# Sliding-window attention and a spectral mix on one core: q and k with nine buffers each, their loads two slots further up in the DMA order

## The chip, the core and the metric

The kernel runs on one core of one Trainium2 chip. The time is device microseconds (us) of one launch, from the first to the last instruction and what lies around them. Several runs are summed up by their median. One execution was taken by the hardware profiler; its engines are named PE (matmuls; PEld is its weight load), DVE, ACT, POOL, and SP, which here only issues DMAs.

## What is computed

q, k and v have the shape (8 batches, 8 heads, 576 positions, 64), in float32. The reference, cut to what matters:

```python
scores = scale * np.matmul(q, k.transpose(0, 1, 3, 2))
mask = (rel >= 0) & (rel < 128)                     # rel = query position - key position
scores = np.where(mask, scores + bias[None], -1e9)  # bias = -slope[head] * |rel|
attn = softmax(scores)
x = np.matmul(attn, v)                              # then heads side by side: (8, 576, 512)
X = np.fft.rfft(x, axis=1)                          # the lowest 64 modes are kept
Yr[m] = Xr[m] @ w_r[m] - Xi[m] @ w_i[m]             # one 512 x 512 pair of weights per mode
Yi[m] = Xr[m] @ w_i[m] + Xi[m] @ w_r[m]
u = x + np.fft.irfft(Y, n=576, axis=1)
out = u + np.maximum(u @ w_ch, 0.0)
```

w_r and w_i have 64 x 512 x 512 float32 values each, 67.1 MB apiece: they are most of what is read from memory.

## The kernel before, in words

**The units.** Two heads fill 128 channels, which the code calls group s (0 to 3). One unit is a group of one batch; there are 32 units, and they are worked in 16 pairs. Pair d holds units 2d and 2d+1. Of each unit q, k and v are loaded by one DMA each (288 KB), so a pair has six loads, called q0, q1, k0, k1, v0, v1 for pair 0 and so on up to q30, q31, k30, k31, v30, v31 for pair 15.

**The slots.** The attention runs in slots n = 0, 1, 2, ...; slots 2d and 2d+1 are those of pair d (`_slot`). A slot makes scores (line 427), exponentials (433) and the mask product (441) of its pair, transposes parts of the pair after it (377, copied out at 387), has POOL cast raw loads of the pair two further on to bf16 (`_cast`, line 367: q in the even slot, k and v in the odd one), and finishes the product with v of the pair before (458, normalised at 476). A cast is the last reader of a raw load; when it is done the load's buffer is free.

**The weights.** After slot 10 the spectrum of group 0 is known, and the products of group 0 with the weights are put between the slots (`_modes`, line 663): 22 tiles of three modes (one has one mode), in order 0 to 21. Each tile has two DMAs (w_r and w_i, 768 KB each, line 611). Tile 0 has a place of its own ("spare"); the others use a ring of three places (`RING`, "wring"). The DMA of tile i has to wait until PE has finished tile i-3. From tile 22 on the weights are those of groups 1 to 3 (line 620, one DMA of 1.5 MB each; products at line 694), in the same ring, until the last stretch of the kernel, which computes the output (lines 728 to 870).

**The order of the DMAs.** All 249 DMAs are issued by SP, one after the other, in the order in which the code calls them: `_load(g, d)` for q, k and v, `_send(g)` for weights. An instruction on SP that waits holds back everything behind it. SP waits for three things: for a free buffer (a POOL cast for q, k and v; PE for weights), and, in every DMA from the ninth on, for the DMA eight places earlier to have landed, since there are eight completion semaphores in turn. So at most eight DMAs are under way.

`_load(g, d)` issues q and k of pair d and v of pair d-1. Before the slots, q and k are called up to pair 7 and v up to pair 6. From slot 8 on, each even slot n calls one more: slot 8 calls q and k of pair 8 with v of pair 7, slot 10 those of pair 9 with v of pair 8, slot 12 those of pair 10 with v of pair 9, and so on. `_send` is called at the end of each slot. From slot 10 on this gives the SP order below (the first weights are of tile 4, which wait for PE to finish tile 1 at the end of slot 10):

```
q18 q19 k18 k19 v16 v17 | tile 4: w_r w_i | q20 q21 k20 k21 v18 v19 | tile 5: w_r w_i | q22 q23 ...
```

q and k have seven buffers each (`QK`, line 24), v has five (`VB`). Load q(i) takes the buffer of q(i-7), load v(i) that of v(i-5).

Of the kernel before, what the change touches and what calls it, by code (L numbers as in the profile page):

```python
# [19 lines left out]
LA = 8  # L20
RING = 3
ROWS = 3
VB = 5
QK = 7
BUSY = 12
TAIL = 2

# [6 lines left out]
def kernel(  # L34
# [16 lines left out]
    g = Ctx()  # L51
# [8 lines left out]
    N = len(units)  # L60
    g.first = [units.index((j, grp[0], 0)) for j, grp in enumerate(GROUPS)] + [N]
    tiles = []
    for grp in GROUPS[:1]:
        mg = ROWS // len(grp)
        n = NM // mg
# [31 lines left out]
    with tc.manual_schedule(engines={ET.SP, ET.PE, ET.Activation, ET.DVE, ET.Pool}):  # L97
        with ExitStack() as wctx:
            wpool = wctx.enter_context(tc.tile_pool(name="wpool", bufs=1))
            g.wring = wpool.tile([P, RING, 2 * ROWS * DM], FP32)  # L100
            g.line = [(j, *t) for j in range(len(GROUPS)) for t in tiles[j]]
            g.sent, g.used = 1, 0
            mctx = ExitStack()
            g.mpsum = mctx.enter_context(
                tc.tile_pool(name="mpsum", bufs=1, space=bass.MemoryType.PSUM, side="right"))
            with ExitStack() as actx:
                cp = actx.enter_context(tc.tile_pool(name="const", bufs=1))
                for j, grp in enumerate(GROUPS[:-1]):
                    g.X[j] = cp.tile([P, len(grp), 3, B, NM], BF16, name=f"X{j}")
                g.mask = cp.tile([P, H, 512], BF16)  # L110
                g.vns = [cp.tile([P, 2 * ST, 2, 72], BF16, name=f"vn{i}") for i in range(2)]
                g.qpool = actx.enter_context(tc.tile_pool(name="qk", bufs=QK))
                g.vpool = actx.enter_context(tc.tile_pool(name="v", bufs=VB))
                g.work = actx.enter_context(tc.tile_pool(name="work", bufs=2))
                g.ps2 = actx.enter_context(
                    tc.tile_pool(name="ps2", bufs=1, space=bass.MemoryType.PSUM))
                g.ps1 = actx.enter_context(
                    tc.tile_pool(name="ps1", bufs=2, space=bass.MemoryType.PSUM))

                loaded = (g.first[1] + LA) // 2  # L120
                for d in range(loaded):
                    _load(g, d)
                    if loaded - 2 <= d:
                        _send(g, 1)
                n1 = H - 1
                with tc.tile_pool(name="tmpc", bufs=1, side="right") as tp:
                    _consts(g, tp)
                    for d in range(2):
                        for w in range(3):
                            _cast(g, d, w)  # L130
                        if d == 0:
                            _consts2(g)
                    for w in range(2):
                        for part in range(2):
                            _tr(g, 0, w, part)
                            _evac(g, 0, w, part, nc.vector if w == 1 else None)
                    nc.scalar.activation(g.one, g.one, AF.Exp, scale=-1.0)
                    _mask(g, 0)
                    for n in range(n1):
                        _slot(g, n, [], [])  # L140
                start = g.first[1] + 2
                with tc.tile_pool(name="spare", bufs=1, side="right") as sp:
                    _load_w(g, 0, sp.tile([P, 2 * ROWS * g.DM], FP32, name="spare"))
                    _send(g, 1)
                    for n in range(n1, start + 1):
                        if g.first[1] <= n and n % 2 == 0 and 2 * loaded <= N:
                            _load(g, loaded)
                            loaded += 1
                        _slot(g, n, [], tiles[0][:1] if n == start else [])
                zx = ctx.enter_context(tc.tile_pool(name="zx", bufs=1, side="right"))  # L150
                g.ZTa = zx.tile([P, 4, 4, 2, 16, 8], FP32)

                _modes(g, *tiles[0][1])
                _send(g)
                counts = [0, 1, 0, 1, 0, 1, 0, 1, 1, 0, 1] + [1] * (N - start - 12) + [1, 1, 1, 1]
                work, todo = {}, list(tiles[0][2:])
                for n in range(start + 1, N + 2 + TAIL):
                    work[n] = [todo.pop(0) for _ in range(counts[n - start - 1])]
                assert not todo
                for n in range(start + 1, N + 2 + TAIL):  # L160
                    if g.first[1] <= n and n % 2 == 0 and 2 * loaded <= N:
                        _load(g, loaded)
                        loaded += 1
                    w = work[n]
                    h = (len(w) + 1) // 2
                    _slot(g, n, w[:h], w[h:])
                    _send(g)
                    if N - 7 <= n < N - 3:
                        _load_wch(g, n - N + 7)
                    if N - 2 <= n < N + 2:  # L170
                        _cast_wch(g, n - N + 2)
            zp = ctx.enter_context(tc.tile_pool(name="zpool", bufs=1, side="right"))
            g.ZT = g.ZTa.bitcast(BF16).rearrange("p e k a m (b t) -> p e k (a m) b t", t=2)[..., 0]
            g.hl = zp.tile([P, len(g.seq), 2, DM], BF16)
            g.Z = zp.tile([P, B, DM], BF16)
            g.ZW = zp.tile([P, B, DM], BF16)
            last = len(GROUPS) - 1
            with ExitStack() as xctx:
                xt = xctx.enter_context(tc.tile_pool(name="xts", bufs=2))
                xps = xctx.enter_context(  # L180
                    tc.tile_pool(name="xps", bufs=2, space=bass.MemoryType.PSUM))
                eps = xctx.enter_context(
                    tc.tile_pool(name="eps", bufs=1, space=bass.MemoryType.PSUM))
                ftq = _ft_steps(g, xt, xps)
                g.Xz = {}
                _expand(g, 0, xt, xps)
                k, xT = 0, _xt(g, 0, xt, xps)
                for i in range(NM - 4):
                    m, w = divmod(i, 2)
                    m *= 2  # L190
                    _pair(g, m, w)
                    _send(g)
                    if i % MB == 1:
                        _expand(g, m // MB + 1, xt, xps)
                    while k < len(g.seq) and k * (NM - 4) < (i + 1) * len(g.seq):
                        nxt = _xt(g, k + 1, xt, xps) if k + 1 < len(g.seq) else None
                        _xw(g, k, xT, xps)
                        xT, k = nxt, k + 1
                    if i >= 4 and ftq:
                        ftq.pop(0)()  # L200
                    if 0 <= i - (NM - 14) < B:
                        _z_early(g, i - (NM - 14), eps)
            g.fps = ctx.enter_context(
                tc.tile_pool(name="fps", bufs=3, space=bass.MemoryType.PSUM))
            g.mm, g.y = {}, {}
            for i in range(3):
                _known(g, i)

            wps = mctx.enter_context(
                tc.tile_pool(name="wps", bufs=1, space=bass.MemoryType.PSUM))  # L210
            g.idle = wps.tile([P, DM], FP32)
            for m in (NM - 4, NM - 2):
                for w in range(2):
                    _pair(g, m, w, BUSY)
                    _send(g)
            mctx.close()
        _finish(g)
# [120 lines left out]
        for c in range(4) for a, z in ((0, 512), (512, S))]  # L338


def _load(g, d):


    N = len(g.units) // 2
    for w, (pool, src) in enumerate(((g.qpool, g.q), (g.qpool, g.k), (g.vpool, g.v))):
        at = d if w < 2 or d == 0 else d - 1
        if at >= N or w == 2 and d == 1:
            continue
        _, s, b = g.units[2 * at]
        if at not in g.two:  # L350
            u = g.two[at] = Ctx()
            u.raw, u.b, u.T, u.att = [[], [], []], [None] * 3, [None] * 3, {}
        u = g.two[at]
        for e in range(2):
            t = pool.tile([P, g.R, g.D], FP32, tag="qkv"[w], name=f"{'qkv'[w]}{2 * at + e}")
            g.nc.sync.dma_start(
                out=t.rearrange("p r d -> p (r d)"),
                in_=src[b + e, 2 * s : 2 * s + 2].rearrange("h (p r) d -> (h p) (r d)", r=g.R))
            u.raw[w].append(t)
# [541 lines left out]
```

## Time and profile before

| What | us |
|---|---|
| median of 3 runs | 443.56 |
| lowest and highest of them | 443.05, 444.04 |
| the profiled execution's own time | 443.07 |
| its span, first to last instruction | 441.3 |

| Engine | busy us | share of the span |
|---|---|---|
| PE | 314.4 | 71% |
| PEld | 207.7 | 47% |
| DVE | 220.4 | 50% |
| ACT | 213.9 | 48% |
| POOL | 103.3 | 23% |

| DMA | MB | us from issue to landing, median |
|---|---|---|
| weights of group 0, 768 KB each | 33.6 | 8.1 to 8.9 |
| weights of groups 1 to 3, 1.5 MB each (the last one in halves) | 100.7 | 10.1 |
| q, k and v, 288 KB each | 28.3 | 6.6 to 6.7 |
| all, read and written | 173.73 | |

The span cut into 40 slices has a digit for the busy share of each engine in each slice; for DMA the digit is the mean share of the core's 16 DMA engines. The chain that ended last goes back from the last instruction to what released it, step by step; of it DMA holds 53%, PE 19%, ACT 15%, DVE 9%. A DMA's time from issue to landing holds the time in which it stood behind others, so a long landing is no slow transfer.

### The profile page before, as it was taken

The numbers are of one execution on the slowest core, as the hardware profiler recorded it, in microseconds if no ns is written. First come the engines' busy times: TensorE is split into PE (matmuls) and PEld (weight loads), VectorE is DVE, ScalarE is ACT, GpSimd is POOL, SyncE is SP. The second block draws the span as 40 slices with busy tenths as digits, with TensorE's granted clock in tenths as the row PEclk, the third lists the DMA queues.
The fourth block names the chain that finished last, engine by engine and source line by source line (L and its number), as shares of the span: only waits on it lengthen the run. The fifth ranks groups of instructions, "written<-read, shape, count | busy, mean of one in ns | idle before, by whom it ended". The sixth has DMA issues, their size and how long they took to land.

```text
span 441.3 us, 10917 instructions
## 1 busy us (share of the span) xinstructions
PE 314.4 (71%) x4624; PEld 207.7 (47%) x4652; DVE 220.4 (50%) x404; ACT 213.9 (48%) x332; POOL 103.3 (23%) x156
## 2 busy tenths in 40 slices
PE   2677788888979878457565656645576487778994
PEld 1455567666757655233333333333343255534552
DVE  6566767787747733342333324233232444512884
ACT  4799879999959603222323212222122232312883
POOL 8745535555524102000000000000000000000982
PEclk9989888999969856877867656568556889969998
DMA  8999979999999999999999999999999999993787
GB/s 288 392 393 394 403 288 403 406 405 407 404 406 405 404 419 416 418 429 427 429 429 429 420 418 423 427 426 428 430 427 429 429 427 420 429 420 140 288 310 263
DMA packets 46145, 173.73 MB, mean 394 GB/s; under 512 B 3984, under 2 KB 3984, under 8 KB 38032
## 3 DMA queue, kind: packets, MB, share of 16 engines
q1 hardware_dynamic: 46096, 173.03, 97.3%
q8 instruction: 36, 0.59, 0.5%
q14 instruction: 13, 0.11, 0.1%
HBM read 163.58 MB, written 9.44 MB: 392 GB/s over the span
## 4 chain that ended last, share of the span: by engine, by line
DMA 53%; PE 19%; ACT 15%; DVE 9%; issue 3%; SPq 0%; POOL 0%; ACTq 0%; POOLq 0%
DMA wring<-in_moe_w_i_dram 29%; DMA wring<-in_moe_w_r_dram 23%; ACT att L433 6%; ACT T L387 5%; PE acc L694 4%; DVE att L441 3%; PE mm L728 2%; PE sc L427 2%; DVE x_sb L476 2%; PE y L728 2%; PE tqk L377 2%; PE av L406 2%; PE acc L663 1%; PE av L458 1%; ACT mask L293 1%
## 5 line engine op out<-in xcount | busy, mean ns | idle before, releaser
L745 ACT CAST hl<-xw 64x512 bf16<-64x512 f32 x72 | 41.8, 580 | 140.1 <-PE xw L741 105.5
L694 PE MATMUL acc<-Xz,wring 128*128 128x32 bf16 x1536 | 51.5, 183 | 68.5 <-DMA wring<-in_moe_w_i_dram 36.6
L694 PEld LDWEIGHTS <-wring 128*128 128x128 bf16 x1536 | 45.5, 101 | 100.7 <-DMA wring<-in_moe_w_i_dram 54.9
L746 DVE TENSOR_TENSOR hl<-xw,hl 64x512 bf16<-64x512 f32 x72 | 49.6, 689 | 79.0 <-ACT hl L745 78.9
L867 POOL TENSOR_TENSOR o<-r,ys 128x512 f32<-128x512 f32 x18 | 22.5, 1277 | 240.2 <-DVE r L859 238.8
L433 ACT ACTIVATE att<-sc 128x1024 bf16<-128x1024 f32 x64 | 69.0, 1077 | 9.7 <-PE sc L427 9.1
L441 DVE TENSOR_TENSOR att<-att,mask 128x1024 bf16<-128x1024 bf16 x64 | 53.6, 838 | 36.8 <-ACT att L433 36.1
L387 ACT COPY T<-tqk 128x640 bf16<-128x640 bf16 x92 | 67.9, 801 | 2.1 <-PE tqk L377 2.1
L741 PE MATMUL xw<-wch,xT 128*128 128x512 bf16 x119 | 49.3, 533 | 4.7 <-issue 3.1
L377 PE MATMUL tqk<-ident_b,b 128*128 128x128 bf16 x432 | 41.1, 240 | 11.5 <-POOL b L367 6.4
L377 PEld LDWEIGHTS <-b 128*128 128x128 bf16 x432 | 29.1, 107 | 23.5 <-issue 11.4
L721 DVE COPY xT<-tp 128x512 bf16<-128x512 bf16 x36 | 15.1, 420 | 35.8 <-PE tp L719 35.6
L367 POOL CAST b<-v 128x576 bf16<-128x576 f32 x32 | 27.0, 868 | 20.0 <-issue 14.3
L427 PE MATMUL sc<-T,T 64*128 64x256 bf16 (+2 forms) x320 | 27.4, 269 | 2.8 <-ACT att L433 1.4
L367 POOL CAST b<-q 128x576 bf16<-128x576 f32 x32 | 21.9, 714 | 28.8 <-issue 28.8
L741 PEld LDWEIGHTS <-xT 128*128 128x128 bf16 x144 | 18.2, 132 | 22.0 <-issue 18.5
L458 PE MATMUL av<-vn,att 128*128 128x65 bf16 (+1 forms) x576 | 25.8, 206 | 0.4 <-DVE vn L410 0.3
L406 PE MATMUL av<-ident_b,T 128*128 128x128 bf16 x160 | 15.9, 236 | 13.8 <-DVE x_sb L476 7.7
L367 POOL CAST b<-k 128x576 bf16<-128x576 f32 x32 | 22.0, 716 | 12.7 <-POOL b L367 7.1
L458 PEld LDWEIGHTS <-att 128*128 128x128 bf16 (+1 forms) x576 | 21.7, 108 | 3.5 <-issue 0.2
L663 PE MATMUL acc<-X,wring 128*128 128x16 bf16 x488 | 18.9, 193 | 5.6 <-DMA wring<-in_moe_w_i_dram 4.1
L476 DVE TENSOR_TENSOR x_sb<-av,rec 128x512 bf16<-128x512 f32 x32 | 22.1, 692 | 1.1
(104 smaller groups left out, 416.7 us busy)
## 6 DMA issues: line engine op xcount, KB each, us to landing
wring<-in_moe_w_r_dram SPq DMA_DIRECT2D x32, 1536.0 KB, 10.1
wring<-in_moe_w_i_dram SPq DMA_DIRECT2D x31, 1536.0 KB, 10.1
wring<-in_moe_w_i_dram SPq DMA_DIRECT2D x22, 768.0 KB, 8.9
wring<-in_moe_w_r_dram SPq DMA_DIRECT2D x20, 768.0 KB, 8.1
q<-in_q_dram SPq DMA_DIRECT2D x32, 288.0 KB, 6.7
k<-in_k_dram SPq DMA_DIRECT2D x32, 288.0 KB, 6.6
v<-in_v_dram SPq DMA_DIRECT2D x32, 288.0 KB, 6.6
out_dram<-o SPq DMA_DIRECT2D x32, 256.0 KB, 2.8
```

What stands on the lines that cost most here:

```text
L367: g.nc.gpsimd.tensor_copy(u.b[w][:, :, e], u.raw[w][e])
L377: g.nc.tensor.transpose(u.tp[:, r - r0], u.b[w][:, r].rearrange("p u d -> p (u d)"), g.ident_b)
L387: copy(u.T[w].rearrange("c h (p r) -> c (h p) r", r=g.R)[:, :, r0:r1], u.tp[:, 0 : r1 - r0].rearrange("c r p -> c p r"))
L427: nc.tensor.matmul(sc[:, e, c0 : c0 + nq], lhsT=kT[es, h, _start(kt) : _start(kt) + P], rhs=qT[es, h, kt * P : kt * P + nq], start=True, s ...
L433: nc.scalar.activation(a, sc, AF.Exp, scale=1.0 / math.sqrt(g.D))
L441: nc.vector.tensor_tensor(out=a, in0=a, in1=m, op=ALU.mult)
L458: nc.tensor.matmul(av[o, h, t * (D + 1) : (t + 1) * (D + 1)], lhsT=u.att[min(kt // 2, 1), h][:, f, c0 : c0 + m], rhs=vn[:, g.ST * h + kt, ...
L476: nc.vector.tensor_tensor(out=xo, in0=avv[:, :, 0:4, 0:D], in1=rec[:, :, 0:4].unsqueeze(-1).broadcast_to([P, 2, 4, D]), op=ALU.mult)
L694: nc.tensor.matmul(acc[:, et, :, m - c0 : m - c0 + 2, :], lhsT=w[:, a].bitcast(BF16)[:, 1::2][:, et * P : (et + 1) * P], rhs=X[:, a, 1 - k ...
L741: nc.tensor.matmul(xw, lhsT=xT[:, dt], rhs=g.wch[:, dt], start=(dt == 0 and g.way[n] != "q"), stop=(dt == 3))
L745: nc.scalar.copy(g.hl[hi, n, h], xw[hi])
L746: nc.vector.tensor_tensor(out=g.hl[lo, n, h], in0=xw[hi], in1=g.hl[hi, n, h], op=ALU.subtract)
```

## The change

q and k get nine buffers each in place of seven. `_load` gets a third argument that says which of q, k and v it issues. The slots from 8 to 10 call `_load` as before; at slot 10 (`start`) q and k of pair 10 are issued as well. From slot 12 on, an even slot n issues v of pair n/2+3, as before, and then q and k of pair n/2+5 in place of those of pair n/2+4.

```diff
-QK = 7
+QK = 9
...
                     for n in range(n1, start + 1):
-                        if g.first[1] <= n and n % 2 == 0 and 2 * loaded <= N:
-                            _load(g, loaded)
-                            loaded += 1
+                        if g.first[1] <= n and n % 2 == 0:
+                            _load(g, n // 2 + LA // 2)
+                            if n == start:
+                                _load(g, n // 2 + LA // 2 + 1, (0, 1))
                         _slot(g, n, [], tiles[0][:1] if n == start else [])
...
                 for n in range(start + 1, N + 2 + TAIL):
-                    if g.first[1] <= n and n % 2 == 0 and 2 * loaded <= N:
-                        _load(g, loaded)
-                        loaded += 1
+                    if n % 2 == 0:
+                        _load(g, n // 2 + LA // 2, (2,))
+                        _load(g, n // 2 + LA // 2 + 1, (0, 1))
...
-def _load(g, d):
+def _load(g, d, which=(0, 1, 2)):
...
     for w, (pool, src) in enumerate(((g.qpool, g.q), (g.qpool, g.k), (g.vpool, g.v))):
         at = d if w < 2 or d == 0 else d - 1
+        if w not in which:
+            continue
```

SP's order after it, from slot 10 on:

```
q18 q19 k18 k19 v16 v17 q20 q21 k20 k21 | tile 4: w_r w_i | v18 v19 q22 q23 k22 k23 | tile 5: w_r w_i | v20 v21 q24 ...
```

Each v stands behind as many DMAs as before. The weights of tiles 4 to 10 stand behind four more. From v28 on (after q30, q31, k30, k31, which are the last of q and k) the order is the old one again. The instructions of PE, DVE, ACT and POOL are the same ones in the same order, and SP issues the same 249 DMAs.

## The prediction, made before the changed kernel was run

> **What bounds the kernel now.** I read the slices of the page first, then the windows by stage, then, where the DMA rate falls, windows of 1 us with the timelines of SP and PE. The page's slices:
>
> ```profile
> DMA  8999979999999999999999999999999999993787
> GB/s 288 392 393 394 403 288 403 406 405 407 404 406 405 404 419 416 418 429 427 429 429 429 420 418 423 427 426 428 430 427 429 429 427 420 429 420 140 288 310 263
> ```
>
> DMA is full (9) from the start to slice 36, with one hole: slice 6, 55 to 66 us, 288 GB/s. The windows by stage (columns: length, busy us and number of PE, PEld, DVE, ACT, POOL, then granted clock, DMA share, GB/s):
>
> ```profile
> 0.00:59.00 59.00, 39.24 (x508) 28.24 (x509) 39.20 (x76) 48.09 (x67) 36.58 (x64) 0.94 1.01 376
> 59.00:66.00 7.00, 5.66 (x101) 4.63 (x99) 3.83 (x9) 4.20 (x6) 2.15 (x4) 0.80 0.63 226
> 66.00:125.00 59.00, 49.26 (x915) 38.93 (x912) 44.12 (x81) 54.74 (x76) 30.99 (x43) 0.96 1.05 404
> 125.00:151.00 26.00, 24.18 (x441) 19.07 (x437) 17.14 (x34) 21.79 (x32) 8.53 (x12) 0.88 1.05 405
> 151.00:403.00 252.00, 165.23 (x2358) 98.60 (x2387) 88.54 (x164) 59.53 (x108) 2.47 (x16) 0.72 1.00 421
> 403.00:441.30 38.30, 30.79 (x319) 18.22 (x318) 27.53 (x43) 25.58 (x46) 22.54 (x18) 0.97 0.69 248
> ```
>
> From 66 to 403 us the DMA share is 1.00 to 1.05, so 1.05 is a full queue: the kernel ends when all bytes are in, plus 38 us of output. No engine is that full: ACT, the fullest between 66 and 125, has 54.74 of 59. An idle us of DMA ahead of 403 is then a us of the kernel, if nothing later gives it back. The hole, in windows of 1 us:
>
> ```profile
> 60.00:61.00 1.00, 0.96 (x19) 0.79 (x19) 0.98 (x1) 1.00 (x2) 0.66 (x2) 1.00 1.05 389
> 61.00:62.00 1.00, 0.12 (x4) 0.02 (x1) 1.00 (x4) 0.23 (x1) 0.00 (x0) 1.00 0.90 332
> 62.00:63.00 1.00, 0.82 (x24) 0.78 (x24) 0.97 (x4) 0.00 (x0) 0.00 (x0) 1.00 0.42 161
> 63.00:64.00 1.00, 1.00 (x32) 0.95 (x30) 0.10 (x1) 0.03 (x1) 0.00 (x0) 0.60 0.11 44
> 64.00:65.00 1.00, 1.00 (x12) 0.75 (x9) 0.00 (x0) 0.94 (x2) 0.00 (x0) 0.50 0.00 0
> 65.00:66.00 1.00, 0.85 (x11) 0.58 (x8) 0.43 (x1) 1.00 (x2) 0.86 (x2) 0.50 0.88 258
> ```
>
> SP's waits between 59 and 64 us have one entry, and SP's timeline the issue that follows it:
>
> ```profile
> SPq L611 <- PE acc L663: 4.5, 1, 4.5
> ...
> 57.96 1.33 SPq L356 DMA_DIRECT2D v<-in_v_dram  x2
> 63.93 0.38 SPq L611 DMA_DIRECT2D wring<-in_moe_w_r_dram  x1
> ```
>
> After v17 (issued at 58.76) SP stands before tile 4's weights until PE has done tiles 0 and 1 (62.18 to 63.93); PE waited for the spectrum of group 0 (DVE, line 527). The loads behind could go, but SP is in order, and the queue runs dry.
>
> **The change, part by part.**
>
> *Four loads into the hole.* q20, q21, k20 and k21 now stand ahead of tile 4's weights: 4 x 288 KB = 1.18 MB, at the 404 GB/s of 66 to 125 us 2.92 us of a full queue. They can go: each waits for the load eight places earlier, which in this stretch lands some 5.8 us after its issue, so they go at about 59.4 to 61.7. The last of SP's old rows went at the same pace (1.33 us for two). Nine buffers matter here: with seven, k21 would take the buffer of k14, whose cast POOL begins only at 65.14; with nine it takes that of k12, cast by 55.0. Tile 4 goes at 63.93 as before, since PE's side is untouched.
>
> How much of the 2.92 us is gained? From above: all of it, if each engine's hole is as long. The 1 us windows give a mean of 0.15+0.63+0.94+1.05+0.17 = 2.94 us below 1.05 (over 1.05: 2.8). From below, by landings: v17 lands 5.8 after 58.76, at 64.6; tile 4's w_r, issued at 63.93, lands 5.0 later, at 68.9. Of these 4.3 us, its own 0.786 MB take 1.95 at 404 GB/s. So the last of the 16 engines stood still for only 2.4 us, and the loads fill that and push the weights 0.5 us. I take 2.6, near the lower end, since a DMA is waited for until its last part is in. The Trainium skill, "DMA: Bandwidth & Descriptors", section "Why a DMA increments its semaphore by 16 and not by 1", says that up to 16 engines finish independently and only the full count means that all data landed. By it the sum is 2.4, by the windows' mean 2.8; the slow fall of the share (0.90, 0.42, 0.11, 0.00) agrees.
>
> *Weights of tiles 4 to 10 behind four more loads.* The bytes ahead of them grow by what the hole takes in, so they land when they did, at most 2.92 - 2.4 = 0.5 us later. What hides this: between 64 and 121 us neither PE nor PEld has one wait for a DMA. The closest is tile 10: w_i issued at 107.95 lands 8.6 later, at 116.6, and PE uses it at 117.50; 0.9 us of cover against 0.5. Cost 0. Were the whole 2.92 us on top, PE would stand 2 us there.
>
> *From v28 on the order is the old one, with 1.18 MB less ahead.* There the gain appears. PE's timeline:
>
> ```profile
> 122.82 0.19 PE L663 MATMUL acc<-X,wring 128*128 128x16 bf16 x1 [1.50 <-DMA wring<-in_moe_w_r_dram]
> 124.78 0.80 PE L663 MATMUL acc<-X,wring 128*128 128x16 bf16 x23 [1.77 <-DMA wring<-in_moe_w_i_dram]
> ```
>
> PE stands 3.27 us for tile 11 (issued 116.63, landed 8.1 later). This wait takes the whole 2.6, so attention and products after it move up 2.6 us too, and with them the releases of the ring (line 611, waits on PE) that pace the weights from 125 on. Between 125 and 151 DMA stays at 1.05 only because of what is queued; both sides move by the same, so it does. From 151 on SP, DMA and the output shift as a whole.
>
> *v in its old place, with full-queue time gained.* v19 takes v14's buffer, whose cast ends at 68.51. Before, SP came there after q20 to k21; now it comes right after v18, at about 65.5, and holds q22 to k23 and tile 5 behind it for 3 us. v21 (cast of v16 by 76.31), v23 (84.18), v25 (92.05), v27 (100.38) likewise. Cover: tile 4's two weights, 3.9 us of bytes, are queued in front. In the old trace w_i of tile 4 lands at 70.8 (6.4 after 64.40); v18 and v19 follow at 0.73 us each, so v19 is due at 72.3. Issued at 68.53, it needs at least 2.8 us (the first load of the kernel, alone in an empty queue): 71.3. Spare 1.0 us. Cost 0.
>
> *The early part.* SP waits 9.9 us in all for POOL at line 356, 3.6 of it between 66 and 125. Nine buffers take away part of the 6.3 before, where DMA stands at 1.05 anyway: 0. The number of DMAs, 249, and SP's 0.33 to 0.5 us for each are the same.
>
> **Sum.** Own time 443.07 (span 441.3 and 1.8 around it) - 2.6 = 440.5; the median of the runs is 0.5 above the profiled execution, so 441.0.
>
> **The rivals.**
>
> *Half the gain.* Compute doesn't follow beyond tile 11: releases after 125 us stay where they were, and the queue, 2.6 us shorter, runs dry. For: SP waits up to 4.5 us for PE there. In the trace tile 12's place is freed at 130.92 and what was issued before lands at 135.8; 2.6 less is 133.2, and 130.92 + 3.0 (the 5.0 of tile 4's w_r less its own 1.95) + 1.95 = 135.9 against the 135.1 due: about 1 us lost, 442.0. Against: PE's 3.27 us wait lies ahead of it.
>
> *The loads don't go into the hole.* If the eighth-earlier rule or a buffer holds q20 to k21 until about 63.9, nothing changes: 443.5. For: eight loads are only 5.8 us of queue. Against: the landings above.
>
> *Slower: v holds SP until the queue is dry.* Place: v19, v21, v23, v25, v27. It decides when a cast comes over 1.0 us later than now, or a restart costs 1 us more than the 2.8; each us beyond loses five times, so from 0.5 us on it outweighs the 2.6. At 1 us: 443.5 - 2.6 + 5 = 445.9. For: restarting took 3.0 us besides the bytes at 63.93, which leaves v19 just 0.1 us (68.53 + 3.0 + 0.73 = 72.3). Against: there the queue was empty, here it isn't.
>
> **How the numbers follow.** Forecast 0.66 (441.0, own range 440.2 to 441.6), half 0.11, no effect 0.12, slower 0.11. Runs differ by some 0.2%, 0.9 us, which I take as the bound of no change: faster 0.77, same 0.12, slower 0.11. The range runs from 440.1 (all 2.92 us, runs 0.5 apart) to 443.6 (no effect); the slower case stays out.
>
> **What would show it.** SP's timeline has four more q and k ahead of the issue at 63.9; the DMA share of 59 to 66 us rises from 0.63 to about 1.0. Tile 11's wait on PE falls from 3.3 to under 1 us, the last weights land near 400.3 in place of 402.9, and the output takes 38 us again. Wrong: a 1 us window under 0.9 after one of the five v stops or after 128 us, PE waiting for tiles 5 to 10, or the hole unfilled.

## The result and the profile after

| | before | after |
|---|---|---|
| median of 21 runs each, us | 443.18 | 441.89 |
| lowest and highest | 441.93, 444.42 | 440.69, 443.71 |
| ratio after to before | | 0.9978, 95% interval 0.9968 to 0.9987 |
| span of the profiled execution, us | 441.3 | 440.0 |

The change makes the kernel faster by 0.22%, 1.0 us (0.6 to 1.4) by the ratio; the two medians lie 1.3 us apart. The direction is the one forecast, the size is not: 2.6 us were forecast. (The forecast of 441.0 starts from 443.56, the median of 3 runs; of 21 runs it is 443.18.) The page's slices for DMA, after the change:

```profile
DMA  8999999999999999999999999999999999993787
GB/s 289 395 390 399 404 379 370 405 406 407 403 406 403 406 422 406 417 427 429 428 427 433 428 426 421 424 421 426 430 423 428 429 423 425 427 421 127 287 312 264
```

The hole in slice 6 is gone from the busy digits. In GB/s it is not: slice 6 moves 379 and slice 7 (66 to 77 us) 370, where the kernel before had 403 in slice 7. The windows by stage (length, busy us and number of PE, PEld, DVE, ACT and POOL, granted clock, DMA share, GB/s), after:

```profile
59.00:66.00 7.00, 5.66 (x101) 4.57 (x98) 3.83 (x9) 4.20 (x6) 2.21 (x4) 0.81 1.02 367
66.00:125.00 59.00, 50.83 (x948) 40.34 (x945) 44.42 (x82) 55.69 (x79) 30.84 (x43) 0.96 1.04 398
125.00:151.00 26.00, 24.07 (x427) 18.55 (x425) 19.06 (x36) 22.10 (x31) 8.42 (x12) 0.89 1.05 405
151.00:403.00 252.00, 165.44 (x2357) 98.07 (x2385) 87.57 (x162) 58.17 (x106) 2.46 (x16) 0.72 1.00 418
```

From 59 to 66 us the rate rises from 226 to 367 GB/s; from 66 to 125 it falls from 404 to 398, and 6 GB/s over 59 us are 0.35 MB, 0.9 us of a full queue. Windows of 2 us show where:

```profile
68.00:70.00 2.00, 2.00 (x38) 1.53 (x39) 1.13 (x4) 1.52 (x3) 1.05 (x2) 0.50 1.05 406
70.00:72.00 2.00, 1.96 (x42) 1.62 (x39) 1.20 (x2) 1.64 (x3) 0.62 (x2) 0.96 0.99 349
72.00:74.00 2.00, 0.78 (x10) 0.52 (x9) 1.94 (x3) 2.00 (x4) 1.49 (x4) 1.00 0.99 336
74.00:76.00 2.00, 1.90 (x39) 1.57 (x41) 1.27 (x4) 1.89 (x4) 0.89 (x2) 1.00 1.02 364
76.00:78.00 2.00, 1.74 (x42) 1.42 (x42) 1.79 (x4) 2.00 (x4) 1.30 (x2) 1.00 1.05 405
```

Nearly all of it lies in 70 to 76 us: 350 GB/s there, against 404 in the kernel before, 0.32 of the 0.35 MB. The whole window, before and then after:

```profile
70.00:76.00 6.00, 4.64 (x90) 3.70 (x87) 4.36 (x7) 5.50 (x9) 2.92 (x5) 1.00 1.04 404
```

```profile
70.00:76.00 6.00, 4.64 (x91) 3.70 (x89) 4.41 (x8) 5.53 (x8) 2.99 (x5) 0.99 1.00 350
```

The share stays at 0.99 to 1.02: by the busy digits alone nothing is wrong. SP's timeline, after:

```profile
63.87 0.38 SPq L614 DMA_DIRECT2D wring<-in_moe_w_r_dram  x1
64.34 0.43 SPq L614 DMA_DIRECT2D wring<-in_moe_w_i_dram  x1
64.87 3.94 SPq L359 DMA_DIRECT2D v<-in_v_dram  x2
68.86 0.90 SPq L359 DMA_DIRECT2D q<-in_q_dram  x2
69.80 0.90 SPq L359 DMA_DIRECT2D k<-in_k_dram  x2
70.81 0.60 SPq L614 DMA_DIRECT2D wring<-in_moe_w_r_dram  x1
```

And from the view of SP's waits between 64 and 70 us, where the columns are the waits' sum in us, their number and the longest:

```profile
SPq L359 <- POOL b L370: 3.1, 1, 3.1
```

SP issues v18 at 64.87 and then stands, 3.1 us before v19, which goes at 68.47, when POOL's cast of v14 ends (68.44). Nothing is put into the queue in that time. The loss begins 1.5 us after SP goes on. PE's wait for tile 11, after:

```profile
121.36 0.19 PE L666 MATMUL acc<-X,wring 128*128 128x16 bf16 x1
123.09 0.89 PE L666 MATMUL acc<-X,wring 128*128 128x16 bf16 x23 [1.54 <-DMA wring<-in_moe_w_i_dram]
```

It is 1.5 us in place of 3.3, and PE goes on at 123.09 and not at 124.78: 1.7 us sooner.

### The profile page after: what moved, and what is told of

Read it like the earlier page. It is cut to its first block, busy times and chain, and to the rows that moved or that the text cites. A ratio compares the mean times of both kernels' runs of the same rounds, so it can differ in the third digit from the quotient of the medians.

```text
span 440.0 us, 10903 instructions
## 1 busy us (share of the span) xinstructions
PE 315.1 (72%) x4624; PEld 207.4 (47%) x4652; DVE 221.3 (50%) x404; ACT 213.9 (49%) x332; POOL 102.8 (23%) x156
## 4 chain that ended last, share of the span: by engine, by line
DMA 51%; PE 21%; ACT 14%; DVE 9%; issue 3%; SPq 0%; POOL 0%; ACTq 0%; POOLq 0%
DMA wring<-in_moe_w_i_dram 30%; DMA wring<-in_moe_w_r_dram 21%; ACT att L436 5%; ACT T L390 5%; PE acc L697 4%; DVE att L444 3%; PE mm L731 2%; PE y L731 2%; PE sc L430 2%; DVE x_sb L479 2%; PE xw L744 2%; PE acc L666 2%; PE tqk L380 2%; PE av L409 1%; PE av L461 1%
## 5 line engine op out<-in xcount | busy, mean ns | idle before, releaser
L444 DVE TENSOR_TENSOR att<-att,mask 128x1024 bf16<-128x1024 bf16 x64 | 54.7, 855 | 36.3 <-ACT att L436 35.6
```

What stands on the lines that cost most here:

```text
L444: nc.vector.tensor_tensor(out=a, in0=a, in1=m, op=ALU.mult)
```

## How far each landing moved

The completion records of the trace give, for each DMA, when each of the 16 engines had its part in. Below is how far a landing moved against the kernel before, in us (mean of the 16 parts / last part), in one execution of each kernel. "Tile 24" is the first weights that wait for PE to be done with tile 21. The last columns are the span and the ratio to the kernel before with its 95% interval. The experiments of the next section stand in the same table.

```text
kernel               GB/s 70-76  tile 5 w_i    tile 20 w_i   tile 24 mean  last weights   span   ratio
before               404          0             0             0             0             441.3  1
after                350         +1.18/+1.76   -1.77/-1.18   -1.57         -1.43/-1.12   440.0  0.9978 (0.9968 to 0.9987)
e1_again (the same)  386         +0.22/+1.80   -2.68/-1.66   -1.75         -1.81/-1.80   439.5  0.9967 (0.9954 to 0.9979)
e6_all_but_12        359         +0.90/+1.62   -2.08/-1.32   -1.09         -0.97/-0.84   440.4  0.9973 (0.9959 to 0.9986)
e2_v7                407         +0.26/+0.44   -2.70/-2.50   -2.52         -2.18/-2.30   439.5  0.9960 (0.9948 to 0.9972)
e3_v_behind          407         +0.20/+0.06   -2.70/-2.74   -2.63         -2.44/-2.79   439.3  0.9950 (0.9937 to 0.9963)
e5_only_12           407         +0.19/+0.23   -2.38/-3.06   -2.60         -2.58/-2.82   438.5  0.9955 (0.9939 to 0.9971)
e8_six_loads         408         +1.42/+1.76   -2.44/-3.00   -2.70         -2.66/-2.72   438.5  0.9947 (0.9935 to 0.9960)
e7_two_loads         405         -0.42/-0.20   -1.92/-1.77   -1.87         -1.18/-1.42   439.9  0.9968 (0.9957 to 0.9979)
e4_nine_alone        406         -0.56/-0.72   -0.57/-0.52   -0.59         -0.48/-0.76   441.0  0.9994 (0.9984 to 1.0004)
```

By the mean landing of v17, all of them are within 0.25 us of the kernel before. But the moment at which PE lets tile 4's weights go, and with it the length of the hole, differs between executions: 63.93 us in the kernel before, 62.66 to 63.86 in the others. So e4_nine_alone, whose order is the old one, is 0.5 us ahead from tile 4 on (63.36); differences of that size say nothing, and what the table shows as gained may be too large by as much.

## The experiments

All are compared with the kernel before on the same chip. Theory A: SP's stop at v19 lets the queue, filled just before, run low, and that costs part of the gain. Theory B: the loss at 70 to 76 us is one lagging engine of one execution.

**e1_again**: the changed kernel, unaltered.

> The changed kernel, unaltered, for a second profile. Both theories: ratio to before 0.997 to 0.999 (0.9978 measured). Theory A (v19 holds SP from 65.3 to 68.5 us and the queue, filled just before, runs shallow from 70 to 76): the windows of 1 us from 70 to 76 again move 340 to 370 GB/s and not 404, and tile 5's weights land about 1.1 us later than in the trace of before. Theory B (the loss there is one lagging DMA engine of one execution): the dip is elsewhere or absent.

The dip is there again and milder: 380 and 372 GB/s at 70 to 74 us, and 405 at 74 to 76, where 340 to 370 were expected throughout. Over the whole window:

```profile
70.00:76.00 6.00, 4.59 (x91) 3.73 (x89) 4.41 (x9) 5.90 (x9) 4.16 (x6) 1.00 1.02 386
```

The mean of tile 5's landing moved by 0.2 us only, not 1.1, but its last part came 1.8 us late, as in the first profile (1.76). So the place is the same in both executions, and how the loss spreads over the 16 engines is not.

**e2_v7**: no long wait for a buffer of v.

```diff
-QK = 9
-VB = 5
+QK = 8
+VB = 7
```

> The changed kernel with eight buffers for q and k and seven for v: v19 then waits for v12's cast (56 us) and not for v14's (68.5). Theory A: SP no longer stops at v19; 70 to 76 us move 395 GB/s or more; tile 5's weights land at 77.1 and 79.0, as before the change, plus at most 0.5; the kernel is some 0.9 us faster than the changed one: ratio about 0.996. Theory B: no change against the changed kernel, 0.9978.

The window has no dip:

```profile
70.00:76.00 6.00, 4.61 (x91) 3.76 (x89) 4.53 (x9) 5.89 (x9) 4.13 (x6) 1.00 1.05 407
```

Tile 5's last part comes 0.44 us later, as expected, and the ratio is 0.9960. The window speaks against theory B, by which it would have stayed near 350 to 386. The ratio alone doesn't decide: its interval, 0.9948 to 0.9972, holds the 0.9967 of e1_again. This kernel also has one buffer less for q and k; e3_v_behind and e5_only_12 keep nine.

**e3_v_behind**: v behind q and k, in all even slots from 12 on; buffers as changed.

```diff
-                        _load(g, n // 2 + LA // 2, (2,))
                         _load(g, n // 2 + LA // 2 + 1, (0, 1))
+                        _load(g, n // 2 + LA // 2, (2,))
```

> The changed kernel with the two loads of v behind the four of q and k in each even slot from 12 on. Theory A: SP's stop at v19 now has 1.18 MB more queued in front of it, so 70 to 76 us stay near 400 GB/s, and the kernel is some 0.9 us faster than the changed one: ratio about 0.996. Theory B: 0.9978.

407 GB/s, and 0.9950: the 0.996 expected lies within its interval. The same DMAs with the same buffers, two of them four places further back, bring 2.2 us where the change brought 1.0 to 1.5. SP's timeline of this kernel:

```profile
64.34 0.43 SPq L614 DMA_DIRECT2D wring<-in_moe_w_i_dram  x1
64.83 1.69 SPq L359 DMA_DIRECT2D q<-in_q_dram  x2
66.57 0.90 SPq L359 DMA_DIRECT2D k<-in_k_dram  x2
67.52 1.28 SPq L359 DMA_DIRECT2D v<-in_v_dram  x2
70.27 0.38 SPq L614 DMA_DIRECT2D wring<-in_moe_w_r_dram  x1
```

q22 to k23 go out while v14 is still being cast, and v19's wait is nearly over when SP comes to it.

**e4_nine_alone**: the kernel before with nine buffers.

```diff
-QK = 7
+QK = 9
```

> The kernel before with nine buffers for q and k, its order as it was. Both theories: the hole of 61 to 66 us stays, ratio 0.999 to 1.001. If the gain came from the buffers alone, 0.998.

0.9994, and the hole stays, 0.6 us shorter since tile 4's weights go at 63.36 in this execution:

```profile
59.00:66.00 7.00, 5.66 (x97) 4.51 (x95) 4.04 (x9) 4.14 (x7) 2.53 (x4) 0.72 0.76 265
```

The buffers alone bring nothing; they only permit the order. Eight do that too (e2_v7, e8_six_loads).

**e5_only_12 and e6_all_but_12**: v behind q and k in slot 12 alone, and in slots 14 and later alone.

```diff
+                        if n == start + 2:
+                            _load(g, n // 2 + LA // 2 + 1, (0, 1))
                         _load(g, n // 2 + LA // 2, (2,))
-                        _load(g, n // 2 + LA // 2 + 1, (0, 1))
+                        if not (n == start + 2):
+                            _load(g, n // 2 + LA // 2 + 1, (0, 1))
```

For e6_all_but_12 the two conditions are exchanged (`n > start + 2`).

> The changed kernel with v18 and v19 behind q22 to k23 in slot 12 alone; later slots as changed. Theory A (the first stop, at v19, behind the refilled hole, is the one that costs): as with v behind in all slots, ratio 0.995 to 0.996, 70 to 76 us at 400 GB/s or more. Rival (every stop at v costs a part): between, about 0.9965, and the weights of tiles 6 to 8 later than those of e3_v_behind by steps.

> The changed kernel with v behind q and k in slots 14 and later, and slot 12 as changed. Theory A: the loss stays, 70 to 76 us at 340 to 385 GB/s, ratio 0.997 to 0.998. Rival (every stop costs): about 0.996.

The window from 70 to 76 us, of e5_only_12 and then of e6_all_but_12:

```profile
70.00:76.00 6.00, 4.61 (x94) 3.60 (x90) 4.99 (x9) 5.89 (x9) 3.81 (x6) 1.00 1.05 407
```

```profile
70.00:76.00 6.00, 4.66 (x76) 3.98 (x76) 4.19 (x8) 5.89 (x8) 3.65 (x5) 0.82 1.01 359
```

The one stop at v19 decides: mended alone, it gives 407 GB/s and 0.9955; with all others mended and this one left, 359 and 0.9973. The two intervals overlap, so the ratios alone don't part them; the windows and the landings do (last weights 2.6 and 1.0 us sooner by the mean). The later stops, v21 and on, cost nothing that can be seen, and the landings of tiles 6 to 8 show no steps: in the changed kernel the mean is 1.2 us behind at tiles 6 and 7 and 1.1 at tile 8, as at tile 5.

This is not because the later stops are shorter. In the changed kernel SP's longest wait, 3.5 us, is the one for v21 (window 71 to 77 us):

```profile
SPq L359 <- POOL b L370: 4.1, 2, 3.5
```

Yet 76 to 82 us move 403 GB/s. What differs is how much is still queued when SP goes on, told by when the DMA ahead lands by the mean of its 16 parts: 3.7 us of transfers at v21, and 2.3 us at v19. The same figure at v19, with the rate of 70 to 76 us behind it, is 2.3 us and 359 GB/s in e6_all_but_12, 2.9 us and 386 in e1_again, 4.1 us and 405 in e7_two_loads (below), 4.7 us and 407 in e2_v7. So the less was left, the deeper the dip; no run varies this depth alone.

**e7_two_loads**: only q goes up; the hole gets half the bytes.

```diff
                             if n == start:
-                                _load(g, n // 2 + LA // 2 + 1, (0, 1))
+                                _load(g, n // 2 + LA // 2 + 1, (0,))
...
-                        _load(g, n // 2 + LA // 2, (2,))
-                        _load(g, n // 2 + LA // 2 + 1, (0, 1))
+                        _load(g, n // 2 + LA // 2, (1, 2))
+                        _load(g, n // 2 + LA // 2 + 1, (0,))
```

> Only q goes up by two slots (q20 and q21 into the hole, 0.59 MB, 1.46 us at 404 GB/s); k stays ahead of v, so SP's stop at v19 has two loads more in front of it than in the changed kernel. If what fills the hole is the gain, byte for byte: 441.3 - 1.4 us of span, ratio 0.9965 to 0.9975, and the DMA share of 59 to 66 us half way between 0.63 and 1.02. If the gain has another source (buffers, order of k): about 0.999 or 0.995.

Span 439.9, ratio 0.9968: 1.4 us, as expected. The share of 59 to 66 us came out at 0.95, higher than half way, since tile 4's weights also started earlier in this execution. In it k20 and k21 stand in front of v19's stop, and there is no dip: half the loads give as much as the changed kernel got out of all four.

**e8_six_loads**: v18 and v19 go into the hole too; eight buffers for q and k, seven for v.

```diff
-QK = 9
-VB = 5
+QK = 8
+VB = 7
...
                             if n == start:
-                                _load(g, n // 2 + LA // 2 + 1, (0, 1))
+                                _load(g, n // 2 + LA // 2 + 1)
...
-                        _load(g, n // 2 + LA // 2, (2,))
-                        _load(g, n // 2 + LA // 2 + 1, (0, 1))
+                        _load(g, n // 2 + LA // 2 + 1)
```

> All six loads of pair 10 and v18, v19 into the hole (1.77 MB, 4.4 us), eight buffers for q and k, seven for v, so that no v waits long. Theory: the hole is 2.4 to 2.9 us, what is left of it (305 GB/s in 64 to 66 us with four loads) is worth at most 0.5 us; the rest pushes tile 4's weights by 1.5 us. Ratio 0.994 to 0.9955. Tile 10 is then needed 0.5 to 1 us before it lands, which the wait for tile 11 takes back. Rival (the wait on tile 10 delays the attention for good): 0.997.

0.9947, the lowest ratio, as expected. Its windows:

```profile
59.00:66.00 7.00, 5.79 (x99) 4.81 (x97) 3.91 (x9) 4.13 (x7) 2.13 (x3) 0.68 1.06 392
70.00:76.00 6.00, 4.58 (x91) 3.73 (x89) 4.38 (x8) 5.89 (x9) 4.20 (x6) 1.00 1.05 408
```

PE then stands 2.3 us for tile 10, more than the 0.5 to 1 expected:

```profile
116.73 0.19 PE L665 MATMUL acc<-X,wring 128*128 128x16 bf16 x1 [0.35 <-DMA wring<-in_moe_w_r_dram]
118.91 0.88 PE L665 MATMUL acc<-X,wring 128*128 128x16 bf16 x23 [1.99 <-DMA wring<-in_moe_w_i_dram]
123.87 1.15 PE L665 MATMUL acc<-X,wring 128*128 128x16 bf16 x24
```

and none for tile 11 (123.87): the wait has moved from one tile to the one before, and the last weights come 2.7 us sooner all the same. The rival, attention delayed for good (0.997), lies outside the interval. Against e3_v_behind the two further loads bring nothing that can be told (0.9947 and 0.9950).

## Why the prediction was right in direction and wrong in size

**Four loads into the hole: right.** In the kernels whose queue stays full after 70 us, tile 20 lands 2.4 to 2.7 us sooner by the mean, and 2.5 to 3.1 by its last part; 2.6 was said, between 2.4 and 2.92. By the ratios, which rest on all runs, e2_v7, e3_v_behind, e5_only_12 and e8_six_loads are 1.8 to 2.3 us below 443.2, and e7_two_loads, with half the bytes, 1.4. So most of the term reaches the end if nothing takes it away. Whether the hole was worth the 2.4 of the lower bound or more, the landings don't decide: in the execution of the kernel before that was profiled, PE let tile 4 go later than in the nine others, and against e4_nine_alone each gain is 0.5 us smaller.

**Weights behind four more loads: right.** Tile 4 lands 0.3 us later, tile 10 at 117.75 by its last part; PE's waits for weights between 64 and 121 us are one of 0.2 us.

**v in its old place, "Spare 1.0 us. Cost 0": this step failed.** The stop was seen where it is (SP held from 65 to 68.5 us), and v19 itself came nearly in time: 72.57 by its last part, where 72.3 was due. What was left out is what stands behind it. I priced the first load after the stop alone, with the time of one load in an empty queue, and took the queue to be full again with it. But six more issues followed from 68.86 to 71.50, each 0.4 to 0.7 us after the one before, into a queue that was short: v19 found 2.3 us of transfers ahead of it by the mean landing of v18 (3.4 by its last part), where v19 before the change, issued at the same time, found 5.0 (6.0). From v19 to tile 5's weights the landings fell back by 0.9 us by the mean (from 2.77 us ahead for v18 to 1.86 ahead for v21) and 1.0 us by the last part. The loss is not v19's alone: v18's 70.80 and the 0.73 us of one load give 71.53 for v19's mean landing, and it landed at 71.79, 0.3 us late; the rest came with the DMAs behind it. The sign that was to show such a stop, a window of 1 us under a share of 0.9, never came: the lowest was 0.92, from 73 to 74 us, and moved 325 GB/s. The rival "v holds SP until the queue is dry" named this place, this wait and a loss of 1 us, but multiplied it by five stops and so came out slower than before. Only the first stop costs (e5_only_12, e6_all_but_12).

**Tile 11's wait takes the gain: right**, for what arrived: 3.27 us became 1.5.

**"From 151 on SP, DMA and the output shift as a whole": not quite.** PE frees tile 21's place 6.1 us after it goes on with what needs tile 20's w_i (160.64 to 166.78 after, 161.82 to 167.95 before): the transforms that make the last spectra (line 520) stand between. SP's weights of tile 24 wait for that, and in all ten traces they are issued 6.20 to 6.23 us after tile 20's last part has landed. So there the last engine's landing counts, not the mean: in the three traces with the dip, tile 20 is 1.8 to 2.7 us ahead by the mean but only 1.2 to 1.7 by its last part, and at tile 24 the mean has fallen back by 0.2 to 1.0 us. The window from 166 to 172 us of the changed kernel, of e6_all_but_12, and of e5_only_12:

```profile
166.00:172.00 6.00, 5.66 (x72) 3.32 (x72) 2.02 (x5) 1.90 (x4) 2.46 (x16) 0.50 0.97 391
```

```profile
166.00:172.00 6.00, 5.63 (x74) 3.29 (x71) 1.88 (x5) 2.02 (x4) 2.46 (x16) 0.50 0.94 356
```

```profile
166.00:172.00 6.00, 5.05 (x63) 2.61 (x61) 2.35 (x6) 1.84 (x4) 1.44 (x10) 0.50 1.00 424
```

The kernel before:

```profile
166.00:172.00 6.00, 5.94 (x71) 3.74 (x70) 2.03 (x5) 1.44 (x3) 2.47 (x16) 0.50 0.99 402
```

The loss of 70 to 76 us is thus paid in two places: bytes not moved then, and, most likely, engines that are ahead standing idle at 168 us until the lagging one is level. The records don't tell the engines apart, but in the changed kernel the first and the last part are 3.7 us apart for the weights before this point (tile 23) and 2.6 us for those behind it (tile 24). The Trainium skill, "DMA: Bandwidth & Descriptors", section "Why a DMA increments its semaphore by 16 and not by 1", says that only the full count of 16 means that all data landed. The traces agree with it: after the change PE goes on with tile 20 at 160.64, when the last part of w_i has landed (160.60), and not at the mean landing (158.28).

Summed for the profiled execution, by the mean landing: 2.77 gained at the hole, 0.91 lost at 70 to 76, 0.09 up to tile 20, 0.20 at 168 and 0.14 after, 1.43 left; the last part of the last weights came 1.1 sooner, and the span is 1.3 shorter. The rival "Half the gain", put at 442.0, was near the number by luck: in it compute doesn't follow, and here compute did. (Its own times give 0.7 us lost, not 1, and so 441.7.)

**What stays open.** The runs show that the stop costs and where. They don't show why a queue that still holds 2.3 us of transfers moves 350 GB/s, nor from what depth on it moves the full rate, nor why the loss falls on all engines in one execution (mean and last part late) and on few in the other (last part only). No run here separates that. Why PE lets tile 4's weights go up to 1.3 us apart in different executions was not looked into either.

## What to carry to other kernels

In this kernel, and as far as one kernel can show: when a hole in the DMA queue is filled with loads from further down, everything behind them reaches its own waits that much sooner: list the next wait in the issue order, and put loads that can go at once ahead of the one that must wait. Price such a stop by what the queue still holds when issuing starts again (2.3 us cost 0.9 here, 3.7 us nothing) and by all the issues that follow it, not by the first. Read GB/s beside the busy share: here the share was 1.00 while a seventh of the rate was missing, and a sign set on the share alone missed it.

## What the runs showed of the hardware that was not expected

- In these traces a queue that runs short is slower before it is empty. From 70 to 76 us the changed kernel's DMA engines are busy 1.00 of the time at 350 GB/s; in the kernels without the dip the same kind of loads run at 1.04 to 1.05 and 404 to 408. The packet records agree: in this window packets of 2304 bytes (one row of q, k or v) take 104 ns on average in the changed kernel, 102 in e6_all_but_12 and 98 in e1_again, and 93 to 94 in the seven traces without the dip.
- The 16 engines drift apart. Between the first and the last part of one load lie 0.7 to 1.6 us in the first 15 us of the kernel before, 2.5 us for the last load before the hole, 1.3 us for the first weights after it, and 3.1 us for those issued at 151 us. So the late ones catch up in the hole. With six loads in it they don't: 2.7 us before and 2.5 after (e8_six_loads).
- A possible part of the drift: the records have 36 instruction fetches of 16 KB, of 0.9 to 1.1 us each in the kernel before, one of them at 65.2 us, near the end of the hole. Whether they make an engine late was not tried.
